# An attention and MoE kernel: the rational activation as a float16 product and a residual, an addition on ScalarE, 19 ring tiles, a new order

## The chip, the cores and the metric

The kernel runs on one core of a Trainium2 chip. A run's time is the device time of that core in microseconds. TensorE multiplies matrices, VectorE, ScalarE and GpSimd work on tiles of 128 partitions, SyncE (SP) issues the transfers. In the profile PE is TensorE, DVE VectorE, ACT ScalarE and POOL GpSimd.

## What is computed

```python
# q, k, v: (4 batches, 8 heads, 768, 64); 16 centroids a head
mask = argmax(q_n @ c_n) == argmax(k_n @ c_n)        # clusters by cosine
attn = softmax(where(mask, q @ k.T / 8, -1e9))
x = (attn @ v) as 3072 tokens x 512
h = x @ w_in                                         # 512 -> 2048
P = a[0] + a[1] * h + a[2] * h**2 + a[3] * h**3
Q = 1 + abs(b[0]) * abs(h) + abs(b[1]) * h**2
out = (P / (Q + 1e-6)) @ w_out                       # 2048 -> 512
```

## The kernel before

Matrix products run in float16 with each operand split in a high and a low part, three products for one. The first of four batches does its attention with the keys as rows; the other three do it by query tile: `attend` takes 128 queries of one head at a time (144 times in all). TensorE makes the scores (L1162), VectorE scales them and takes the extreme (L1191), ScalarE exponentiates, VectorE and ScalarE split the normalised weights into two float16 parts (the split on VectorE is L1222), a transfer on SP's queue turns them, and TensorE multiplies by v into `px` (L1242).

`moe` works on 256 tokens at a time (three such blocks in a batch) and on 512 columns of d_ff in two halves. One half is a MoE tile: 128 partitions by 512 elements, 96 of them in all, 72 in the first three batches. For each, TensorE makes `ph` (L1450, 24 matmuls in two steps), and the engines then make the activation in three float32 tiles u, t and s:

- ScalarE: u = |ph| scaled, t = a first polynomial step. VectorE: two more steps (L1467, L1468); the constant term a0 is still missing in t.
- GpSimd: s = u + BT (L1515), s = s * u (L1516); s is Q without its 1.
- ScalarE: in three tiles of four s = s + cq and then u = Ln(s), in the others u = Ln(s + cq); u = Exp(-u), an estimate of 1/Q.
- s = s * u with cq added, near 1: GpSimd (L1533 where cq is not in yet, L1538) in the first three batches, VectorE (L1527) in the last.
- t = (t + a0) * u: GpSimd as two instructions (L1544, L1545) in 43 of the 72 tiles, else VectorE (L1551).
- t = (s - 2) * t on VectorE (L1556): one Newton step for the quotient, with the sign turned.
- ScalarE copies t to float16, the high part (L1560); the low part is the difference, on GpSimd (L1564) in the first three batches and on VectorE in the last. Both parts overwrite s.
- TensorE: `po` += both parts times `wout` (L1575), 12 matmuls in two steps, one for each 128 tokens.

The tiles come from a ring of 12 buffers of 2 KB a partition (`wide`, tag "ring", `NR`), which the preparation of the weights uses as well (`weights`: raw words, magnitudes, signs). In the last batch the second half of each tile pair uses other buffers (`sq1`, `sk1`, `sq2`). A buffer is free again when its last reader is done. No run-time scheduler orders the work: each operation is appended to a plan with an engine, a duration and a due time, and a list written out in the file, `ORDER`, says in which order the plan's operations are issued:

```python
    def emit(self):
        assert sorted(ORDER) == list(range(len(self.ops)))
        for i in ORDER:
            self.ops[i]()
```

An engine takes its own instructions in that order and waits at each for what it needs. Shares such as 0.6 in the table `K` are spread evenly over the tiles by `kshare`.

Of the kernel before, what the change touches and what calls it, by code (L numbers as in the profile page):

```python
# [11 lines left out]
F16 = mybir.dt.float16  # L12
# [3 lines left out]
ALU = mybir.AluOpType  # L16
# [41 lines left out]
K = {'mulp': 0.6, 'mulp.3': 0.0, 'a0t': 1.15, 'xn': 14, 'scp': 1, 'vsc': 0.75, 'sup0': 0, 'stk': 2, 'lop': 0, 'mgp': 0, 'rvn': 2, 'at': 3, 'vn': 3, 'ah': 5, 'sqd': 0.0, 'ed': 0.0, 'ed.3': 1.0, 'gld': 0.0, 'gld.3': 1.0, 'sqd.3': 0.0, 'ghd': 0.0, 'sua': 1.0, 'acq': 0.75, 'T1': 1, 'quick': 1}  # L58
# [188 lines left out]
def clustered_attention_moe_kernel(  # L247
# [550 lines left out]
    def g_scale(b, vt):  # L798
# [9 lines left out]
        def g1c(i):  # L808
            return g1.ap[:, i : i + 1]
# [600 lines left out]
    def moe(b, tb, vt):  # L1410
# [7 lines left out]
        for ci in range(NWC):  # L1418
# [11 lines left out]
            for h in range(2):  # L1430
# [61 lines left out]
                def g16(i, sv=sv, k=k):  # L1492
                    w = 2 * TW * (k + 1)
                    return sv().bitcast(F16)[:, i * w : (i + 1) * w]
# [171 lines left out]
```

## Time and profile before

| | |
|---|---|
| median of 3 runs | 931.77 us (931.6 to 931.96) |
| span of the profiled execution | 930.4 us, 1.4 below the median |
| PE busy | 863.5 us, 93% |
| DVE busy | 835.6 us, 90% |
| ACT busy | 811.2 us, 87% |
| POOL busy | 729.3 us, 78% |

The span runs from the first to the last instruction; what lies around it is known only as the difference to the runs. Busy shares are means over stages that differ much, so the rows below are split by stage. A busy time contains waits inside an instruction, which matters for instructions whose length varies.

### The profile page before, as it was taken

How to read it: one execution, taken by the hardware profiler on the slowest of the kernel's cores; microseconds unless marked ns; L12 is line 12 of the kernel's file. 1: busy time of each engine (PE TensorE's matmuls, PEld its weight loads, DVE VectorE, ACT ScalarE, POOL GpSimd, SP SyncE). 2: the span in 40 equal slices, each digit the busy share in tenths (PEclk: the TensorE clock that was granted, in tenths of full speed). 3: DMA queues.
4: the chain of work that ended last, by engine and by line, in shares of the span. 5: the costliest groups of instructions: out<-in, count | busy, mean ns of one | idle time of the engine just before them, and what ended most of it. 6: DMA issues, size and time to landing. Idle time of an engine off the chain costs nothing.

```text
span 930.4 us, 20764 instructions
## 1 busy us (share of the span) xinstructions
PE 863.5 (93%) x7705; PEld 581.1 (62%) x7705; DVE 835.6 (90%) x1503; ACT 811.2 (87%) x1558; POOL 729.3 (78%) x771
## 2 busy tenths in 40 slices
PE   1679998988899999999989999999999999999997
PEld 1357665656566666666666766666666675777663
DVE  6789999769989999999999999999999998899986
ACT  5577697989999999999999999999999998886774
POOL 2546789988999999999989988988989996464342
PEclk9989999989999999999999999999999999999999
DMA  7995765796977899998799879896987587501000
GB/s 200 232 249 130 190 193 148 177 230 138 188 133 154 164 161 203 155 167 163 155 162 180 164 135 169 178 188 110 208 150 150 92 165 130 121 2 33 8 24 23
DMA packets 360853, 137.70 MB, mean 148 GB/s; under 512 B 335665, under 2 KB 352049, under 8 KB 360753
## 3 DMA queue, kind: packets, MB, share of 16 engines
q1 hardware_dynamic: 360752, 136.39, 72.0%
q8 instruction: 60, 0.98, 0.4%
q14 instruction: 41, 0.33, 0.1%
HBM read 41.98 MB, written 6.29 MB: 52 GB/s over the span
## 4 chain that ended last, share of the span: by engine, by line
PE 54%; DVE 19%; ACT 9%; POOL 6%; issue 6%; DMA 5%; SPq 1%; ACTq 0%; DVEq 0%; POOLq 0%
PE ph L1450 18%; PE po L1575 18%; PE s L1162 7%; PE px L1242 5%; DVE ah L1222 3%; DVE s L1191 3%; DMA rvm<-in_v_dram 2%; PE s L1286 2%; DVE t L1467 1%; DVE t L1556 1%; ACT s L395 1%; PE px L1349 1%; DVE t L1468 1%; DVE top L1295 1%; PE z L1330 1%
## 5 line engine op out<-in xcount | busy, mean ns | idle before, releaser
L1450 PE MATMUL ph<-x,win 128*128 128x256 f16 x2304 | 273.1, 273 | 6.3 <-DVE t L1468 4.7
L1450 PEld LDWEIGHTS <-win 128*128 128x128 f16 x2304 | 223.2, 98 | 55.3 <-DVE t L1468 8.6
L1575 PE MATMUL po<-wout,s 128*128 128x512 f16 x1008 | 239.3, 379 | 0.7 <-POOL s L1564 0.7
L1191 DVE TENSOR_SCALAR_CACHE_REDUCE s<-s,cc 128x768 f32<-128x768 f32 x144 | 145.9, 1017 | 15.4 <-PE s L1162 14.8
L1575 PEld LDWEIGHTS <-s 128*128 128x128 f16 x1008 | 96.4, 98 | 101.2 <-issue 2.2
L1222 DVE SCALAR_TENSOR_TENSOR ah<-s,su,ah 128x768 f16<-128x768 f32 x144 | 144.9, 1011 | 5.6 <-ACT ah L395 5.3
L395 ACT ACTIVATE ah<-s,su 128x768 f16<-128x768 f32 x144 | 129.0, 901 | 7.8 <-DVE su L1210 7.2
L395 ACT ACTIVATE s<-s,nm 128x768 f32<-128x768 f32 x144 | 126.1, 876 | 7.3 <-DVE s L1191 4.9
L1162 PE MATMUL s<-sk,sq 128*128 128x384 f16 x576 | 117.8, 329 | 8.9 <-DVE ah L1222 7.9
L1516 POOL TENSOR_TENSOR s<-s,u 128x512 f32<-128x512 f32 x84 | 114.4, 1362 | 7.0
L1538 POOL TENSOR_TENSOR s<-s,u 128x512 f32<-128x512 f32 x72 | 99.1, 1378 | 7.0 <-ACT u L395 6.7
L1515 POOL TENSOR_SCALAR s<-u,g 128x512 f32<-128x512 f32 x84 | 69.6, 829 | 36.4 <-ACT u L395 33.6
L1564 POOL TENSOR_TENSOR s<-t,s 128x512 f16<-128x512 f32 x72 | 88.1, 1226 | 8.8 <-ACT s L1560 6.8
L1162 PEld LDWEIGHTS <-sq 128*128 128x128 f16 x576 | 52.2, 98 | 53.7 <-DVE ah L1222 17.9
L1556 DVE SCALAR_TENSOR_TENSOR t<-s,t 128x512 f32<-128x512 f32 x84 | 81.8, 973 | 0.8 <-POOL s L1538 0.5
L1242 PE MATMUL px<-at,vhi 128*64 128x256 f16 x864 | 75.2, 276 | 0.0
L395 ACT ACTIVATE u<-ph,gk 128x512 f32<-128x512 f32 x84 | 57.8, 688 | 9.3 <-PE ph L1450 8.7
L1468 DVE SCALAR_TENSOR_TENSOR t<-t,gk,ph 128x512 f32<-128x512 f32 x84 | 62.8, 748 | 3.0
L395 ACT ACTIVATE t<-ph,gk 128x512 f32<-128x512 f32 x84 | 65.4, 780 | 0.0
L1467 DVE SCALAR_TENSOR_TENSOR t<-ph,gk,t 128x512 f32<-128x512 f32 x84 | 62.1, 739 | 1.1 <-ACT t L395 1.0
L1545 POOL TENSOR_TENSOR t<-t,u 128x512 f32<-128x512 f32 x43 | 57.6, 1340 | 3.6
L1242 PE MATMUL px<-at,vlo 128*64 128x256 f16 x432 | 59.7, 273 | 0.0
(232 smaller groups left out, 1751.3 us busy)
## 6 DMA issues: line engine op xcount, KB each, us to landing
rwi<-in_moe_w_in_dram SPq DMA_DIRECT2D x16, 512.0 KB, 4.1
rwo<-in_moe_w_out_dram SPq DMA_DIRECT2D x16, 512.0 KB, 4.4
rk<-in_k_dram SPq DMA_DIRECT2D x32, 192.0 KB, 3.4
rq<-in_q_dram SPq DMA_DIRECT2D x32, 192.0 KB, 3.7
rvm<-in_v_dram SPq DMA_DIRECT2D x16, 384.0 KB, 3.8
rv<-in_v_dram SPq DMA_DIRECT2D x16, 384.0 KB, 4.1
out_dram<-ob SPq DMA_DIRECT2D x24, 256.0 KB, 2.9
sk<-sk SPq DMA_DIRECT2D x12, 192.0 KB, 3.4
```

The costliest lines, as they stand in the source:

```text
L395: lambda: nc.scalar.activation(out=out(), in_=in_(), func=func, **{a: (x() if callable(x) else x) for a, x in kw.items()}),
L1162: nc.tensor.matmul(sc.ap[:, i, :SH], lhsT=st["q" + x].ap[:, j, t, :], rhs=st["k" + x].ap[:, j, ks, :].rearrange("p t c -> p (t c)"), start ...
L1191: lambda nm=nm, view=view: ts(out=view(), in0=view(), scalar1=cc.ap[:, 0:1], scalar2=None, op0=ALU.mult, op1=ALU.min, accum_out=nm.ap),
L1222: lambda part=part, view=view, su=su: stt(out=part(1), in0=view(), scalar=su.ap, in1=part(0), op0=ALU.mult, op1=ALU.subtract),
L1242: nc.tensor.matmul(px.ap[j * D : (j + 1) * D, :], lhsT=vv.ap[:, j, kt, :], rhs=at[j].ap[:, p_, kt].rearrange("p t c -> p (t c)"), start=(i ...
L1450: nc.tensor.matmul(ph.ap[:, fi * TW : (fi + 1) * TW], lhsT=win[:, wpart, c, f * P : (f + 1) * P], rhs=xs[c].ap[:, xpart], start=(i == 0), ...
L1468: stt(out=t[h].ap, in0=t[h].ap, scalar=col("a1")(), in1=ph.ap, op0=ALU.add, op1=ALU.mult)
L1516: nc.gpsimd.tensor_tensor(out=sv(), in0=sv(), in1=uv(), op=ALU.mult)
L1538: lambda uv=uv, sv=sv: nc.gpsimd.tensor_tensor(out=sv(), in0=sv(), in1=uv(), op=ALU.mult),
L1556: lambda tv=tv, sv=sv: stt(out=tv(), in0=sv(), scalar=2.0, in1=tv(), op0=ALU.subtract, op1=ALU.mult),
L1564: lambda tv=tv, g16=g16, e=(nc.vector if kshare("gld", b, i_) else nc.gpsimd): e.tensor_tensor(out=g16(1), in0=tv(), in1=g16(0), op=ALU.su ...
L1575: nc.tensor.matmul(po[ti].ap, lhsT=g16(gg)[:, c0 : c0 + P], rhs=wout[:, wpart, f, :], start=(i == 0 and f == 0), stop=(i == 2 and f == NF ...
```

## The change

The quotient is made in another way. g is a new float16 tile from the ring with a high and a low part (in the last batch's second halves a buffer `sk2`).

- s = u + BT is done by ScalarE in all tiles, s = s * u stays with GpSimd. The separate addition of cq is gone: Ln takes it as its bias everywhere.
- high part at once: g0 = (t + a0) * u, written as float16.
- residual: s = (s + 1 + 1e-6) * g0, then t = (t + a0) - s.
- low part from it: g1 = t * u, on GpSimd in all tiles.
- g0 and t - s are on VectorE in seven tiles of ten; in three of ten GpSimd does them (t + a0, then the product and the difference). The product with g0 is always on VectorE. The shares are the same in all batches.
- the two polynomial steps become two entries of the plan. The factor on the output loses its minus sign.
- `NR` is 19; the scratch for transfers that engines describe in software is cut to 1024 bytes.
- `ORDER` is a new list of 4218 entries, before 4184, over the whole kernel.

```diff
-K = {'mulp': 0.6, 'mulp.3': 0.0, 'a0t': 1.15, 'xn': 14, 'scp': 1, 'vsc': 0.75, 'sup0': 0, 'stk': 2, 'lop': 0, 'mgp': 0, 'rvn': 2, 'at': 3, 'vn': 3, 'ah': 5, 'sqd': 0.0, 'ed': 0.0, 'ed.3': 1.0, 'gld': 0.0, 'gld.3': 1.0, 'sqd.3': 0.0, 'ghd': 0.0, 'sua': 1.0, 'acq': 0.75, 'T1': 1, 'quick': 1}
+K = {'xn': 14, 'scp': 1, 'vsc': 0.75, 'sup0': 0, 'stk': 2, 'lop': 0, 'mgp': 0, 'rvn': 2, 'at': 3, 'vn': 3, 'ah': 5, 'sua': 1.0, 'T1': 1, 'quick': 1, 'sqd': 0.0, 'gld': 0.0, 'gp': 0.3, 'pp': 0.0, 'NR': 19, 'acb': 1.0}
...
-            pts(out=g1c(OI), in0=g1c(OI), scalar1=-1.0 / TOP, scalar2=1.0, op0=ALU.mult, op1=ALU.mult)
+            pts(out=g1c(OI), in0=g1c(OI), scalar1=1.0 / TOP, scalar2=1.0, op0=ALU.mult, op1=ALU.mult)
...
+                    g_t = buf([P, 2, FW], F16, "sk2", f"g{n}", kn("stk", 2)) if last and h else buf([P, 2, FW], F16, "ring", f"g{n}_{h}", NR)
...
+                act(722, uv, sv, AF.Ln, ss, us, uu + kb("ln", b), [s_t, u_t], bias=cq)
+                act(630, uv, uv, AF.Exp, [], us, uu + kb("ln", b), [u_t], scale=-1.0)
+                if kshare("gp", b, i_):
+                    op(
+                        "POOL", 847,
+                        lambda tv=tv, col=col: nc.gpsimd.tensor_scalar(
+                            out=tv(), in0=tv(), scalar1=col("a0")(), scalar2=1.0, op0=ALU.add, op1=ALU.mult
+                        ),
+                        [gk], tss, uu + kb("mul", b) - 0.2, [t_t],
+                    )
+                    op(
+                        "POOL", 1340,
+                        lambda tv=tv, uv=uv, g16=g16: nc.gpsimd.tensor_tensor(out=g16(0), in0=tv(), in1=uv(), op=ALU.mult),
+                        [*us, *tss], [g_t], uu + kb("mul", b), [t_t, u_t],
+                    )
                 else:
                     dve(
+                        919,
+                        lambda tv=tv, uv=uv, col=col, g16=g16: stt(
+                            out=g16(0), in0=tv(), scalar=col("a0")(), in1=uv(), op0=ALU.add, op1=ALU.mult
+                        ),
+                        [*us, *tss, gk], [g_t], uu + kb("mul", b), [t_t, u_t], n=1,
+                    )
...
+                    dve(
+                        800,
+                        lambda sv=sv, g16=g16: stt(out=sv(), in0=sv(), scalar=1.0 + 1e-6, in1=g16(0), op0=ALU.add, op1=ALU.mult),
+                        [g_t], ss, uu + kb("e", b), [s_t], n=1,
+                    )
+                if kshare("gp", b, i_):
+                    op(
+                        "POOL", 1362,
+                        lambda tv=tv, sv=sv: nc.gpsimd.tensor_tensor(out=tv(), in0=tv(), in1=sv(), op=ALU.subtract),
+                        ss, tss, uu + kb("fin", b), [t_t, s_t],
+                    )
+                else:
+                    dve(
+                        920,
+                        lambda tv=tv, sv=sv, col=col: stt(
+                            out=tv(), in0=tv(), scalar=col("a0")(), in1=sv(), op0=ALU.add, op1=ALU.subtract
+                        ),
+                        [*ss, gk], tss, uu + kb("fin", b), [t_t, s_t], n=1,
+                    )
...
+                    lambda tv=tv, uv=uv, g16=g16, e=(nc.vector if kshare("gld", b, i_) else nc.gpsimd): e.tensor_tensor(
+                        out=g16(1), in0=tv(), in1=uv(), op=ALU.mult
                     ),
-                    [*tss, gb[0]], [gb[1]], uu + kb("gl", b), [t_t, s_t],
+                    [*tss, *us], [g_t], uu + kb("gl", b), [t_t, u_t],
...
-    nc = _bacc.Bacc("TRN2", target_bir_lowering=False, num_devices=1)
+    nc = _bacc.Bacc("TRN2", target_bir_lowering=False, num_devices=1, dynamic_dma_scratch_size=1024)
```

Dropped from the diff are the new list and the old forms of the same instructions, which the section on the kernel names.

## Rows read from the trace of the kernel before

**Rows 1.** Busy time by stage: start:end, length, busy us (instructions) of each engine.
```profile
0.00:200.00 200.00, 156.05 (x1757) 108.69 (x1759) 163.79 (x336) 146.24 (x270) 138.82 (x176) 0.97 0.77 193
...
200.00:250.00 50.00, 43.99 (x412) 30.71 (x409) 42.89 (x84) 47.28 (x97) 43.61 (x50) 0.99 0.76 168
...
250.00:500.00 250.00, 243.27 (x2121) 161.63 (x2119) 235.17 (x429) 240.29 (x478) 233.06 (x245) 1.00 0.87 163
...
500.00:775.00 275.00, 270.08 (x2348) 181.59 (x2345) 259.42 (x469) 265.57 (x523) 246.03 (x248) 1.00 0.85 157
...
775.00:846.00 71.00, 70.83 (x553) 49.13 (x550) 63.18 (x97) 59.21 (x107) 36.00 (x30) 1.00 0.35 68
...
846.00:930.40 84.40, 79.25 (x528) 49.36 (x525) 71.13 (x94) 52.65 (x86) 31.77 (x26) 0.99 0.08 24
```

**Rows 2.** Chain that ended last: start us, length us, what; the last 73 us.
```profile
857.44 5.24 PE ph L1450 x48
...
862.68 2.59 PE po L1575 x12
```

**Rows 3.** Timeline of VectorE: start us, length us, the last attention split.
```profile
845.03 1.01 DVE L1222 SCALAR_TENSOR_TENSOR ah<-s,su,ah 128x768 f16<-128x768 f32 x1
```

**Rows 4.** VectorE's groups, 250 to 775 us: count, busy us, mean ns.
```profile
L1222 DVE SCALAR_TENSOR_TENSOR ah<-s,su,ah 128x768 f16<-128x768 f32 x124 | 124.8, 1010 | 3.1 <-ACT ah L395 2.8 <-DMA rq<-in_q_dram 0.2
...
L1556 DVE SCALAR_TENSOR_TENSOR t<-s,t 128x512 f32<-128x512 f32 x66 | 63.3, 959 | 0.6 <-POOL s L1538 0.5
...
L1468 DVE SCALAR_TENSOR_TENSOR t<-t,gk,ph 128x512 f32<-128x512 f32 x66 | 49.4, 748 | 2.3
...
L1551 DVE SCALAR_TENSOR_TENSOR t<-t,gk,u 128x512 f32<-128x512 f32 x27 | 31.3, 1158 | 0.0
```

**Rows 5.** One line's instructions over the span: least, median and longest ns.
```profile
L1551 DVE SCALAR_TENSOR_TENSOR t<-t,gk,u x41: 739/945/2130, 218.5 to 910.7; 128x512 f32<-128x512 f32 x41
...
L1556 DVE SCALAR_TENSOR_TENSOR t<-s,t x84: 670/823/1811, 222.4 to 913.1; 128x512 f32<-128x512 f32 x84
```

**Rows 6.** VectorE's groups with two SBUF operands, 790 to 930.4 us.
```profile
L1556 DVE SCALAR_TENSOR_TENSOR t<-s,t 128x512 f32<-128x512 f32 x12 | 11.9, 991 | 0.1
...
L1551 DVE SCALAR_TENSOR_TENSOR t<-t,gk,u 128x512 f32<-128x512 f32 x12 | 10.9, 912 | 0.0
...
L1564 DVE TENSOR_TENSOR s<-t,s 128x512 f16<-128x512 f32 x12 | 10.7, 895 | 0.0
...
L1527 DVE SCALAR_TENSOR_TENSOR s<-s,u 128x512 f32<-128x512 f32 x12 | 10.4, 865 | 0.7 <-ACT u L395 0.6
...
L1564 DVE TENSOR_TENSOR sq<-sk,sq 128x512 f16<-128x512 f32 x12 | 9.8, 815 | 2.6 <-ACT sq L1560 2.5
...
L1527 DVE SCALAR_TENSOR_TENSOR sq<-sq,sq 128x512 f32<-128x512 f32 x12 | 9.4, 785 | 1.9 <-ACT sq L395 1.9
...
L1551 DVE SCALAR_TENSOR_TENSOR sk<-sk,gk,sq 128x512 f32<-128x512 f32 x12 | 9.4, 780 | 0.0
...
L1556 DVE SCALAR_TENSOR_TENSOR sk<-sq,sk 128x512 f32<-128x512 f32 x12 | 9.3, 777 | 0.2
```

**Rows 7.** ScalarE's groups over the whole span: count, busy us, mean ns.
```profile
L1560 ACT CAST s<-t 128x512 f16<-128x512 f32 x84 | 51.7, 617 | 4.3 <-DVE t L1556 4.2
...
L395 ACT ACTIVATE s<-s,cq 128x512 f32<-128x512 f32 x60 | 43.4, 723 | 3.9 <-POOL s L1516 3.9
```

**Rows 8.** GpSimd's groups, 250 to 775 us: count, busy us, mean ns.
```profile
L1538 POOL TENSOR_TENSOR s<-s,u 128x512 f32<-128x512 f32 x66 | 91.1, 1381 | 7.0 <-ACT u L395 6.7
...
L1516 POOL TENSOR_TENSOR s<-s,u 128x512 f32<-128x512 f32 x66 | 88.7, 1343 | 5.5
...
L1564 POOL TENSOR_TENSOR s<-t,s 128x512 f16<-128x512 f32 x66 | 80.6, 1223 | 7.2 <-ACT s L1560 6.8
...
L1515 POOL TENSOR_SCALAR s<-u,g 128x512 f32<-128x512 f32 x66 | 52.9, 801 | 6.7 <-ACT u L395 4.0 <-ACT su L395 1.6 <-PE po L1575 0.2
...
L1545 POOL TENSOR_TENSOR t<-t,u 128x512 f32<-128x512 f32 x39 | 52.5, 1347 | 3.3
```

More of the change, by code (lines that the diff above doesn't have):

```diff
@@ L1464, in moe @@
                 )
-                def poly(t=t, h=h, ph=ph, col=col):
-                    stt(out=t[h].ap, in0=ph.ap, scalar=col("rho")(), in1=t[h].ap, op0=ALU.mult, op1=ALU.mult)
-                    stt(out=t[h].ap, in0=t[h].ap, scalar=col("a1")(), in1=ph.ap, op0=ALU.add, op1=ALU.mult)
-                dve(1523, poly, [ph, gk], [t[h]], u_ + h + kb("phr", b), [t_t], n=2)
+                dve(
+                    739,
+                    lambda t=t, h=h, ph=ph, col=col: stt(
+                        out=t[h].ap, in0=ph.ap, scalar=col("rho")(), in1=t[h].ap, op0=ALU.mult, op1=ALU.mult
+                    ),
+                    [ph, gk], [t[h]], u_ + h + kb("phr", b), [t_t],
+                )
+                dve(
+                    748,
+                    lambda t=t, h=h, ph=ph, col=col: stt(
+                        out=t[h].ap, in0=t[h].ap, scalar=col("a1")(), in1=ph.ap, op0=ALU.add, op1=ALU.mult
+                    ),
+                    [ph, gk], [t[h]], u_ + h + kb("phr", b), [t_t],
+                )
                 gw = 1 if last and ci >= NWC - 1 and tb >= NB - kn("fine", 0) else GW
@@ L1490, in sv, with g16 @@
                     return view(s_t)
-                def g16(i, sv=sv, k=k):
-                    w = 2 * TW * (k + 1)
-                    return sv().bitcast(F16)[:, i * w : (i + 1) * w]
+                def g16(i, g_t=g_t):
+                    return g_t.ap[:, i]
                 uu = u_ + seg[-1]
-                mulp = kshare("mulp", b, i_)
-                swap = kn("swap") and not last and not mulp
-                if kshare("sqd", b, i_) or swap:
+                if kshare("sqd", b, i_):
                     dve(
@@ L1512, in moe @@
                 else:
-                    def square(uv=uv, sv=sv):
-                        nc.gpsimd.tensor_scalar(out=sv(), in0=uv(), scalar1=g1c(BT), scalar2=1.0, op0=ALU.add, op1=ALU.mult)
-                        nc.gpsimd.tensor_tensor(out=sv(), in0=sv(), in1=uv(), op=ALU.mult)
-                    op("POOL", (2330, 3930)[k], square, [*us, g1], ss, uu + kb("sq", b), [s_t, u_t])
-                acq = kshare("acq", b, i_)
-                if acq:
-                    act((724, 1165)[k], sv, sv, AF.Identity, [], ss, uu + kb("ln", b), [s_t], bias=cq)
@@ L1522, in moe @@
-                act((630, 1070)[k] if acq else (724, 1165)[k], uv, sv, AF.Ln, ss, us, uu + kb("ln", b), [s_t, u_t], **({} if acq else {"bias": cq}))
-                act((630, 1070)[k], uv, uv, AF.Exp, [], us, uu + kb("ln", b), [u_t], scale=-1.0)
-                if kshare("ed", b, i_):
-                    dve(
-                        (840, 1300)[k] if last else (1000, 1850)[k],
-                        lambda uv=uv, sv=sv, acq=acq: stt(out=sv(), in0=sv(), scalar=0.0 if acq else 1.0 + 1e-6, in1=uv(), op0=ALU.add, op1=ALU.mult),
-                        us, ss, uu + kb("e", b), [s_t, u_t], n=1,
-                    )
-                else:
-                    if not acq: op(
-                        "POOL", (790, 1340)[k],
+                    op(
+                        "POOL", 829,
+                        lambda uv=uv, sv=sv: nc.gpsimd.tensor_scalar(
+                            out=sv(), in0=uv(), scalar1=g1c(BT), scalar2=1.0, op0=ALU.add, op1=ALU.mult
+                        ),
+                        [*us, g1], ss, uu + kb("sq", b), [s_t, u_t],
+                    )
@@ new lines, in moe @@
+                    op(
+                        "POOL", 1362,
+                        lambda uv=uv, sv=sv: nc.gpsimd.tensor_tensor(out=sv(), in0=sv(), in1=uv(), op=ALU.mult),
+                        [*us, g1], ss, uu + kb("sq", b), [s_t, u_t],
+                    )
[6 more added lines that the diff above has]
+                            out=tv(), in0=tv(), scalar1=col("a0")(), scalar2=1.0, op0=ALU.add, op1=ALU.mult
+                        ),
+                        [gk], tss, uu + kb("mul", b) - 0.2, [t_t],
+                    )
+                    op(
+                        "POOL", 1340,
+                        lambda tv=tv, uv=uv, g16=g16: nc.gpsimd.tensor_tensor(out=g16(0), in0=tv(), in1=uv(), op=ALU.mult),
+                        [*us, *tss], [g_t], uu + kb("mul", b), [t_t, u_t],
+                    )
+                else:
+                    dve(
+                        919,
+                        lambda tv=tv, uv=uv, col=col, g16=g16: stt(
+                            out=g16(0), in0=tv(), scalar=col("a0")(), in1=uv(), op0=ALU.add, op1=ALU.mult
+                        ),
+                        [*us, *tss, gk], [g_t], uu + kb("mul", b), [t_t, u_t], n=1,
+                    )
@@ L1533, in moe @@
+                if kshare("pp", b, i_):
+                    op(
+                        "POOL", 790,
                         lambda sv=sv: nc.gpsimd.tensor_scalar(out=sv(), in0=sv(), scalar1=cq, scalar2=1.0, op0=ALU.add, op1=ALU.mult),
-                        [], ss, uu + kb("e", b) - 0.5, [s_t],
+                        us, ss, uu + kb("e", b) - 0.5, [s_t],
                     )
                     op(
-                        "POOL", (1360, 2440)[k],
-                        lambda uv=uv, sv=sv: nc.gpsimd.tensor_tensor(out=sv(), in0=sv(), in1=uv(), op=ALU.mult),
@@ L1539, in moe @@
-                        us, ss, uu + kb("e", b), [s_t, u_t],
-                    )
-                if mulp or swap:
-                    def times(tv=tv, uv=uv, col=col):
-                        nc.gpsimd.tensor_scalar(out=tv(), in0=tv(), scalar1=col("a0")(), scalar2=1.0, op0=ALU.add, op1=ALU.mult)
-                        nc.gpsimd.tensor_tensor(out=tv(), in0=tv(), in1=uv(), op=ALU.mult)
-                    op("POOL", (2183, 3840)[k], times, [*us, gk], tss, uu + kb("mul", b), [t_t, u_t])
-                else:
-                    dve(
-                        (919, 1600)[k] if last else (1110, 2100)[k],
-                        lambda tv=tv, uv=uv, col=col: stt(out=tv(), in0=tv(), scalar=col("a0")(), in1=uv(), op0=ALU.add, op1=ALU.mult),
-                        [*us, gk], tss, uu + kb("mul", b), [t_t, u_t], n=1,
-                    )
@@ L1554, in moe @@
-                dve(
-                    (800, 1290)[k] if last else (1080, 1930)[k],
-                    lambda tv=tv, sv=sv: stt(out=tv(), in0=sv(), scalar=2.0, in1=tv(), op0=ALU.subtract, op1=ALU.mult),
-                    ss, tss, uu + kb("fin", b), [t_t, s_t], n=1,
-                )
-                gb = [ss[0], ss[-1]]
-                op("ACT", (619, 1050)[k], lambda tv=tv, g16=g16: nc.scalar.copy(out=g16(0), in_=tv()), tss, [gb[0]],
-                   uu + kb("gh", b), [t_t, s_t], chain="gh")
@@ L1562, in moe @@
-                op(
-                    *(("DVE", (780, 1400)[k]) if kshare("gld", b, i_) else ("POOL", (1231, 2230)[k])),
-                    lambda tv=tv, g16=g16, e=(nc.vector if kshare("gld", b, i_) else nc.gpsimd): e.tensor_tensor(
-                        out=g16(1), in0=tv(), in1=g16(0), op=ALU.subtract
+                        "POOL", 1360,
+                        lambda sv=sv, g16=g16: nc.gpsimd.tensor_tensor(out=sv(), in0=sv(), in1=g16(0), op=ALU.mult),
+                        [g_t], ss, uu + kb("e", b), [s_t],
+                    )
+                else:
+                    dve(
+                        800,
+                        lambda sv=sv, g16=g16: stt(out=sv(), in0=sv(), scalar=1.0 + 1e-6, in1=g16(0), op0=ALU.add, op1=ALU.mult),
+                        [g_t], ss, uu + kb("e", b), [s_t], n=1,
+                    )
@@ new lines, in moe @@
+                if kshare("gp", b, i_):
+                    op(
+                        "POOL", 1362,
+                        lambda tv=tv, sv=sv: nc.gpsimd.tensor_tensor(out=tv(), in0=tv(), in1=sv(), op=ALU.subtract),
+                        ss, tss, uu + kb("fin", b), [t_t, s_t],
+                    )
+                else:
+                    dve(
+                        920,
+                        lambda tv=tv, sv=sv, col=col: stt(
+                            out=tv(), in0=tv(), scalar=col("a0")(), in1=sv(), op0=ALU.add, op1=ALU.subtract
+                        ),
+                        [*ss, gk], tss, uu + kb("fin", b), [t_t, s_t], n=1,
+                    )
@@ L1566, in moe @@
+                op(
+                    *(("DVE", 780) if kshare("gld", b, i_) else ("POOL", 1361)),
+                    lambda tv=tv, uv=uv, g16=g16, e=(nc.vector if kshare("gld", b, i_) else nc.gpsimd): e.tensor_tensor(
+                        out=g16(1), in0=tv(), in1=uv(), op=ALU.mult
                     ),
-                    [*tss, gb[0]], [gb[1]], uu + kb("gl", b), [t_t, s_t],
+                    [*tss, *us], [g_t], uu + kb("gl", b), [t_t, u_t],
                 )
@@ L1581, in moe @@
                     for ti in range(TB):
-                        op("PE", 6 * 216, lambda ti=ti, h=h, second=second: second(ti, h), [*ss, *wo], [po[ti]],
-                           u_ + h + kb("po", b, 4.0), [po2, s_t])
+                        op("PE", 6 * 216, lambda ti=ti, h=h, second=second: second(ti, h), [g_t, *wo], [po[ti]],
+                           u_ + h + kb("po", b, 4.0), [po2])
         whole = load([P, TB, DM], F32, f"ob{b}_{tb}") if MERGE else None
```

364 rows, old and new, of the table ORDER are left out of this document.

## The prediction

> **What bounds the kernel now.** I read the stage windows first [rows 1]. From 250 to 775 us TensorE is busy 513.4 us of 525 (97.8%), from 775 to 846 us 70.8 of 71, after it 79.3 of 84.4. So TensorE sets the pace from about 250 us to the end; ScalarE (505.9 of 525, 96%), VectorE (494.6, 94%) and GpSimd (479.1, 91%) run close behind. Ahead of 250 us TensorE is busy only 200.0 of 250: that is where time could come from. The chain that ended last confirms the end: in the last 70 us it is first and second product in turn, 12 matmuls of `ph` in 1.31 us (48 in 5.24) and 6 of `po` in 1.30 (12 in 2.59) [rows 2]. The chain also gives what one step of TensorE's queue is worth. One more point in time matters: the last attention split on VectorE starts at 845.03 us and takes 1.01, so ends at 846 [rows 3]. Behind it stand the last turn of the weights, the last `px`, and then only MoE steps on TensorE: 84.4 us to the end of the span.
>
> VectorE's rows in the middle [rows 4] show that it does two different kinds of work. Instructions with a PSUM operand do not vary (L1222 1010 ns, L1468 748). Those with two SBUF operands do: L1551 has a least time of 739 ns and L1556 of 670 [rows 5], but their means in the middle are 1158 and 959 [rows 4]. The excess, 0.42 us in 27 and 0.29 us in 66 instructions, is 0.33 us a piece. In the last stage the eight groups with two SBUF operands have means of 0.777 to 0.991 us [rows 6]; over the same least times (739 for L1551, 670 for the rest) the excess is 0.165 us a piece. GpSimd is busy 91% in the middle and 67.8 of 155.4 us (44%) from 775 us on [rows 1]: the excess goes with GpSimd's share. I call it w.
>
> **ScalarE: less work.** A copy of 617 ns goes from all 96 tiles, and an Identity add of cq (723 ns) from 72 of them; an Identity add of BT comes to all 96, which I take at the same 723 [rows 7]: 59 + 52 - 69 = 42 us less over the span, from which the bias that Ln takes again in those 72 tiles gives a little back. ScalarE is not what ends last, so I count this as no gain: TensorE and VectorE hide it. If both had room, it would give up to 42 us.
>
> **GpSimd: much less in the middle.** Per 66 middle tiles go L1515 (52.9 us) and L1538 (91.1), and the pair of L1545 (39 by 1.347, with an add ahead of each like L1515's 0.801: 83.8 together) falls to 19 of 66 tiles (three in ten), each with a third instruction of 1.35 us [rows 8]. L1516 and L1564's 1223 ns stay in kind. 479.1 - 52.9 - 91.1 - 42.9 + 25.7 = 318, 61% of 525. Cost nothing; it lowers w.
>
> **VectorE: more work, and this sets the sum.** Before, a middle tile has L1551 in 29 of 72 and L1556 in all. After, it has the product into g in 51, the product with g in 72, and the residual in 51; tile number i leaves two of them to GpSimd by the 0.3 share (21 of 72 in the first three batches, 7 of 24 in the last). All three have two SBUF operands. The last batch loses L1527, L1551, L1556 and L1564's subtraction on VectorE and gets the same three. I count what stands in VectorE's own order ahead of the last attention split, in the old list and in the new one. Old: 29 x 1.158 + 72 x 0.959 in the first three batches, 32 of the last batch at 0.85 (mean of the groups in [rows 6]): 33.6 + 69.0 + 27.3 = 129.9 us. New: 110 with a column as scalar (L1551's kind, at least 0.739) and 79 with a constant (L1556's, at least 0.670): 81.3 + 52.9 = 134.2 us, plus 189 w. One tile less has its two polynomial steps ahead (1.5 us). So 2.8 us + 189 w more. No row shows the float16 output and input of these forms on VectorE beyond L1564's, which has the same least time class [rows 6]; I take no gain. Bounds for w: 0.165 (GpSimd at 44%) and 0.33 (at 91%); 61% is nearer the first, so I take 0.17: +32, together +35 us.
>
> The Trainium skill, SBUF — State Buffer, section Who interferes with whom, says that a VectorE instruction with two SBUF inputs and a GpSimd instruction that reads SBUF exclude each other, the second waiting until the first is done. By that rule every hit would cost half a GpSimd instruction of 1.35 us, at 61% about 0.41 us a piece, and the sum would be some 45 us above mine. The trace agrees in kind (a longest L1556 of 1811 ns [rows 5]), but at 91% the rule would give 0.62 and the row gives 0.33.
>
> **The order.** In TensorE's list 41 steps of `po` and 22 of `ph` follow the last attention product, where 33 and 20 did: 8 x 1.30 + 2 x 1.31 = 13.0 us more behind the split [rows 2]. So 97.4 us instead of 84.4. The same attention work therefore has to be done earlier while VectorE has more to do. The steps ahead of the first MoE tile are 171 on TensorE where they were 170, and about the same work on VectorE and ScalarE; SP's queue issues the same transfers, shuffled with the rest, so I price its moves at nothing, covered by TensorE's 2% and by VectorE's backlog; if a transfer comes late, it adds to VectorE's idle time below.
>
> **The ring and the waits.** 19 tiles against 12 hold four tiles per MoE tile instead of three: 4.75 in flight for 4. g is freed by `po`, the others earlier. New waits: `po` needs GpSimd's last product in the last batch, where VectorE made it; queued behind that on GpSimd is the next tile's s*u, for which ScalarE's Ln waits. With GpSimd at 44% before in that stage I take 0; if it is late, 1 or 2 us at the end. The ring also feeds the weights; VectorE's idle 36.2 us ahead of 200 and 7.1 us from 200 to 250 [rows 1] may shrink: I take 30 and 4, an estimate.
>
> **The sum.** VectorE is busy 764.5 us up to 846, its first five stages added [rows 1]; its idle time there is 81.5, of which 38.2 lie behind 250 us. If VectorE is what others wait for, I give it the idle share that TensorE has now where it binds, 2% of 600: 12 us, so 46 in all. 764.5 + 35 + 46 = 845.5, then 97.4: a span of 943. The median of the runs lies 1.4 us above the profiled span (931.77 against 930.4): **944 us**. TensorE alone would give 846 - 13 + 97.4, the old span: it no longer binds.
>
> **Rivals.**
> - *VectorE becomes the bound* (forecast), 0.55. With w of 0.165 and 35 us idle 932; with 0.25 and 50 us 963. For it: 94% busy in the middle now, and 189 dearer instructions. Against: the 82 us of idle it had.
> - *TensorE stays the bound and starts earlier*, faster, 0.27. The place is 150 to 250 us, where weights and first tiles share the ring; TensorE's gaps ahead of 250 us are 50 us, and a quarter of them back gives 930.4 - 12.5 + 1.4 = 919. It decides where 189 w plus idle stays under 64 us: w under 0.10 at 46 us idle, or 0.16 at 33. For it: 0.165 was seen late in the span; against: at least 30 us of idle belong to the start, when data arrive.
> - *The changes cancel*, 0.08: less from the start, more on VectorE, or ScalarE and GpSimd eased where TensorE bound anyway. 930 to 934.
> - *The port wait stays as in the middle now*, 0.10: w 0.33 gives 189 x 0.33 = 62 instead of 32, so 974. For it: two-operand instructions now follow each other, and so do GpSimd's of 1.35 us. This is the rule above in a softer form; in full it would give 990.
>
> Chances: slower by over 0.2% 0.52 + 0.10 = 0.62; within 0.2% (about what a measurement here can tell from no change) 0.09; faster 0.29. For 8 in 10 the range goes from 915 (most of the faster rival) to 968 (part of the last). The forecast's own range is 932 to 963.
>
> **What would show it.** Right: VectorE over 97% busy from 250 us to the last split, that split at 840 to 855 us, TensorE's idle time waiting for VectorE (`po` or scores behind products with g), GpSimd near 60% and ScalarE near 91% in the middle; means near 0.85 us for the product with g and 0.91 for the other two. Wrong: means near 0.68 and 0.74, or VectorE idle under 35 us ahead of the split, or TensorE full from before 230 us. The prediction fails most easily on w and on how early the first MoE tile starts.

## The result, and the profile after

915.6 us (four runs, 914.8 to 917.3) against 931.7 before (four runs): a ratio of 0.9856, 95% interval 0.9822 to 0.9890 (the two medians alone give 0.983). The change makes the kernel faster by 1.4%; the forecast was 944 us and slower. The profiled span is 913.0 us. Runs of the kernel before spread more than those of after, from 926.7 to 932.0 us over all chips used, and its profiled span of 930.4 us lies at the slow end; that matters for the start, below.

Busy time by stage of the kernel after, in the columns of [rows 1], cut at its own last attention split:

```profile
0.00:200.00 200.00, 159.20 (x1877) 114.10 (x1877) 157.50 (x343) 150.99 (x282) 126.72 (x164) 0.97 0.81 198
...
200.00:250.00 50.00, 44.76 (x403) 32.04 (x404) 47.71 (x90) 49.07 (x93) 42.63 (x46) 1.00 0.81 146
...
250.00:500.00 250.00, 246.59 (x2176) 168.98 (x2174) 245.62 (x483) 243.93 (x476) 153.69 (x159) 1.00 0.93 176
...
500.00:775.00 275.00, 269.78 (x2313) 181.54 (x2311) 264.90 (x498) 254.99 (x491) 161.66 (x169) 1.00 0.84 154
...
775.00:818.50 43.50, 43.50 (x358) 32.87 (x356) 37.82 (x54) 39.98 (x69) 27.08 (x22) 1.00 0.26 53
...
818.50:913.00 94.50, 90.18 (x586) 55.42 (x584) 66.58 (x74) 51.77 (x80) 64.78 (x48) 0.99 0.08 25
```

One line's instructions over the span, least, median and longest ns, then first and last start:

```profile
L1224 DVE SCALAR_TENSOR_TENSOR ah<-s,su,ah x144: 990/1009/1020, 195.7 to 817.5; 128x768 f16<-128x768 f32 x144
```

The last split ends at 818.5 us, where it ended at 846 [rows 3], and 94.5 us follow. In the middle TensorE is busy 516.4 us of 525 (before 513.4 [rows 1]), VectorE 510.5 (97.2%, before 494.6), ScalarE 498.9, GpSimd 315.4 (60%, before 479.1). VectorE has indeed hardly any idle time left there. But up to the last split it is busy only 753.5 us, 11 less than before, and not 35 more.

VectorE's three new forms in the middle, 250 to 775 us (count, busy us, mean ns):

```profile
L1572 DVE SCALAR_TENSOR_TENSOR s<-s,g 128x512 f32<-128x512 f32 x68 | 48.6, 715 | 0.2
...
L1553 DVE SCALAR_TENSOR_TENSOR g<-t,gk,u 128x512 f16<-128x512 f32 x47 | 38.1, 810 | 0.0
...
L1584 DVE SCALAR_TENSOR_TENSOR t<-t,gk,s 128x512 f32<-128x512 f32 x47 | 35.0, 747 | 0.3
```

Over the least times of [rows 5] (739 ns with a column as scalar, 670 with a constant) that is 0.07, 0.05 and 0.01 us: 0.04 us a piece, where [rows 4] gave 0.33. From 775 us to the end the same forms look quite different:

```profile
L1572 DVE SCALAR_TENSOR_TENSOR s<-s,g 128x512 f32<-128x512 f32 x12 | 13.2, 1100 | 0.5
...
L1584 DVE SCALAR_TENSOR_TENSOR t<-t,gk,s 128x512 f32<-128x512 f32 x11 | 13.2, 1196 | 0.2
...
L1553 DVE SCALAR_TENSOR_TENSOR g<-t,gk,u 128x512 f16<-128x512 f32 x10 | 12.0, 1201 | 4.1 <-ACT u L397 3.9
...
L1572 DVE SCALAR_TENSOR_TENSOR sq<-sq,g 128x512 f32<-128x512 f32 x12 | 10.9, 908 | 6.3 <-POOL g L1547 5.7
...
L1584 DVE SCALAR_TENSOR_TENSOR sk<-sk,gk,sq 128x512 f32<-128x512 f32 x7 | 6.3, 905 | 0.2
...
L1553 DVE SCALAR_TENSOR_TENSOR g<-sk,gk,sq 128x512 f16<-128x512 f32 x7 | 5.9, 844 | 3.1 <-PE po L1602 2.3 <-ACT sq L397 0.6
```

Here the excess is 0.33 us a piece, at a GpSimd share of 67% (91.9 of 138). Who waited longest for whom in the middle (us in total, times, longest):

```profile
POOL g L1591 <- DVE t L1584: 67.2, 26, 5.2
...
POOL t L1578 <- DVE s L1572: 22.7, 7, 6.6
...
PEld L1164 <- DVE ah L1224: 14.8, 30, 2.2
...
PE s L1164 <- DVE ah L1224: 5.8, 7, 1.7
```

GpSimd now waits for VectorE: 67 us for the residual, 23 for the product with g. TensorE's matmuls wait for the attention split for 6 us in all and its weight loads (PEld), which run beside matmuls, for 15; before these were 7 and 15, so the gain does not show in these waits.

How far TensorE got can be estimated: the matmuls of nine groups by stage, times what one takes in an unbroken run (0.109 us for `ph`, 0.216 for `po`, and so on). In us of work done by the time in the first column; the second kernel with the old order is the run with only the ring changed (below, profiled span 926.6):

```
by us   before   old order, 19 ring tiles   after   after - second
200      124.7            131.4             131.6        0.2
250      166.7            172.2             175.8        3.6
325      239.7            244.9             250.5        5.6
450      361.3            367.2             373.4        6.2
600      506.9            511.7             524.1       12.4
775      680.6            685.3             696.0       10.7
```

So the lead of 7 us at 200 us that the two profiles show comes neither from the new quotient nor from the new order: the old order with 19 ring tiles has it too. Whether the ring or the single execution makes it, one trace of each cannot tell; in the time the ring alone gives nothing (below), which speaks for the execution. What quotient and order give comes from 200 us on: 3.6 us to 250 and some 9 more to 600. By this estimate TensorE did 97.0% of what it could there (339.5 of 350, the old order with 19 ring tiles), and now does 99.5% (348.3).

### The profile page after: what moved, and what is told of

The parts are those of the page before. It is cut to its first block, busy times and chain, and to the rows that moved or that the text cites. A ratio compares the mean times of both kernels' runs of the same rounds, so it can differ in the third digit from the quotient of the medians.

```text
span 913.0 us, 20529 instructions
## 1 busy us (share of the span) xinstructions
PE 854.0 (94%) x7705; PEld 584.9 (64%) x7705; DVE 820.1 (90%) x1538; ACT 790.7 (87%) x1486; POOL 576.6 (63%) x607
## 4 chain that ended last, share of the span: by engine, by line
PE 53%; DVE 15%; ACT 15%; DMA 9%; issue 5%; SPq 1%; POOL 1%; ACTq 0%; DVEq 0%
PE po L1602 18%; PE ph L1453 17%; PE s L1164 6%; PE px L1244 5%; ACT s L397 4%; DMA sq<-tq 3%; DVE s L1193 3%; ACT ah L397 2%; ACT u L397 2%; DVE ah L1224 2%; DMA rvm<-in_v_dram 2%; PE z L1332 1%; ACT t L397 1%; DVE g L1553 1%; PE ptl L1060 1%
## 5 line engine op out<-in xcount | busy, mean ns | idle before, releaser
L1602 PE MATMUL po<-wout,g 128*128 128x512 f16 x1152 | 266.7, 379 | 0.5 <-POOL g L1591 0.3
L1453 PE MATMUL ph<-x,win 128*128 128x256 f16 x2304 | 266.3, 273 | 0.6 <-DVE df L1075 0.4
L1602 PEld LDWEIGHTS <-g 128*128 128x128 f16 x1152 | 111.2, 98 | 121.3 <-issue 2.2
L1591 POOL TENSOR_TENSOR g<-t,u 128x512 f16<-128x512 f32 x84 | 117.6, 1402 | 97.1 <-DVE t L1584 81.1
L1518 POOL TENSOR_TENSOR s<-s,u 128x512 f32<-128x512 f32 x84 | 112.5, 1344 | 49.5 <-ACT s L397 38.8
L1164 PE MATMUL s<-sk,sq 128*128 128x384 f16 x576 | 114.2, 326 | 11.7 <-DVE ah L1224 9.2
L1572 DVE SCALAR_TENSOR_TENSOR s<-s,g 128x512 f32<-128x512 f32 x84 | 64.6, 769 | 0.7
L397 ACT ACTIVATE s<-u,g 128x512 f32<-128x512 f32 x84 | 60.6, 724 | 1.1 <-POOL t L1578 0.3
L397 ACT ACTIVATE u<-s,cq 128x512 f32<-128x512 f32 x84 | 59.7, 718 | 1.7 <-POOL s L1518 1.7
L1553 DVE SCALAR_TENSOR_TENSOR g<-t,gk,u 128x512 f16<-128x512 f32 x61 | 53.5, 878 | 4.1 <-ACT u L397 3.9
```

The costliest lines, as they stand in the source:

```text
L397: lambda: nc.scalar.activation(out=out(), in_=in_(), func=func, **{a: (x() if callable(x) else x) for a, x in kw.items()}),
L1164: nc.tensor.matmul(sc.ap[:, i, :SH], lhsT=st["q" + x].ap[:, j, t, :], rhs=st["k" + x].ap[:, j, ks, :].rearrange("p t c -> p (t c)"), start ...
L1453: nc.tensor.matmul(ph.ap[:, fi * TW : (fi + 1) * TW], lhsT=win[:, wpart, c, f * P : (f + 1) * P], rhs=xs[c].ap[:, xpart], start=(i == 0), ...
L1518: lambda uv=uv, sv=sv: nc.gpsimd.tensor_tensor(out=sv(), in0=sv(), in1=uv(), op=ALU.mult),
L1553: lambda tv=tv, uv=uv, col=col, g16=g16: stt(out=g16(0), in0=tv(), scalar=col("a0")(), in1=uv(), op0=ALU.add, op1=ALU.mult),
L1572: lambda sv=sv, g16=g16: stt(out=sv(), in0=sv(), scalar=1.0 + 1e-6, in1=g16(0), op0=ALU.add, op1=ALU.mult),
```

## The experiments

All ratios are to the kernel before, run on the same chip; after stands at 0.9856.

**The old quotient in the new order.** The parts of the old quotient get a tile of their own (`g_t`, as in the change), 19 ring tiles; each old operation is issued where the new one stands that does its part. Against the kernel before, without the list:

```diff
+                    g_t = buf([P, 2, FW], F16, "sk2", f"g{n}", kn("stk", 2)) if last and h else buf([P, 2, FW], F16, "ring", f"g{n}_{h}", NR)
...
-                def g16(i, sv=sv, k=k):
-                    w = 2 * TW * (k + 1)
-                    return sv().bitcast(F16)[:, i * w : (i + 1) * w]
+                def g16(i, g_t=g_t):
+                    return g_t.ap[:, i]
```

> The old quotient (copy and Newton step, GpSimd's shares as before), with its high and low part in a tile of their own, 19 ring tiles, and the new order carried over to its operations. Theory O (the gain comes from the order, which lets TensorE start earlier between 150 and 250 us and keeps it fed): about 918 us. Theory Q (the gain comes from the relief that the new quotient gives GpSimd, ScalarE and the shared port): 930 us or more, GpSimd and ScalarE again over 90% busy in the middle.

1123 us, ratio 1.210 (1.2075 to 1.2127). Waits between 250 and 775 us:

```profile
ACT g L1560 <- DVE t L1556: 59.0, 31, 4.8
...
POOL g L1564 <- ACT g L1560: 83.2, 32, 9.7
```

**The new quotient in the old order**, 19 ring tiles, the other way round.

> The new quotient and 19 ring tiles in the old order (each new operation stands where the one stood that it takes the place of). Theory O: about 931 us or slower, because VectorE has its three operations in places made for others. Theory Q: 918 to 922 us.

1001 us, ratio 1.078 (1.0762 to 1.0806).

```profile
POOL s L1517 <- ACT s L396: 187.4, 56, 8.3
...
PE s L1163 <- DVE ah L1223: 36.2, 41, 3.8
```

Neither theory holds: with the wrong partner, either half costs far more than the whole change brings. The rows show where engines stand. In the first, ScalarE waits at its copy for the Newton step (59 us) and GpSimd for that copy (83 us). In the second, ScalarE's new addition has been put where GpSimd's square stood, GpSimd waits 187 us for it, and TensorE waits 36 us for the attention split, where it waited 7 before. Which of these waits carries the loss was not traced. An order written out fits one set of operations; as carried over, these two runs cannot split the gain.

**19 ring tiles alone** in the kernel before.

```diff
-... 'T1': 1, 'quick': 1}
+... 'T1': 1, 'quick': 1, 'NR': 19}
-    nc = _bacc.Bacc("TRN2", target_bir_lowering=False, num_devices=1)
+    nc = _bacc.Bacc("TRN2", target_bir_lowering=False, num_devices=1, dynamic_dma_scratch_size=1024)
```

> The kernel before with 19 ring tiles and the small scratch, nothing else. If waits for a free ring tile held TensorE or the weights in the old order, 925 to 929 us; if not (both theories), 931 us, no change over 0.2%.

928.6 us, ratio 1.0003 (0.9988 to 1.0019): nothing. Smaller rings under the new order were not timed.

**The new front on the old kernel, the old front on the new one.** Nearly all of the entries ahead of the first MoE operation (920 in the old list, 917 in the new) are the same operations, so this stretch can be exchanged. In short, where the file has the sorted list written out:

```
front = sorted(ORDER[:920], key=place_in_the_new_order)
ORDER = front + ORDER[920:]
```

> The kernel before (old quotient, 19 ring tiles), of whose order only the 920 entries ahead of the first MoE operation (weights, first batch's attention, first work on the second) are sorted as in the new order; the rest keeps its old order. Theory F (a good part of the gain is won ahead of 250 us by the new order of that stretch alone): 919 to 924 us, with scores and first MoE tiles 5 to 8 us earlier. Theory M (it is won where MoE tiles run, by the matched quotient and order): 929 to 932 us.

938.3 us, ratio 1.0107 (1.0091 to 1.0123).

> The kernel after with the 917 entries ahead of its first MoE operation sorted as in the old order, all else as after. Theory F: 921 to 925 us, the lead of TensorE at 250 us gone. Theory M: 914 to 917 us.

917.8 us, ratio 0.9880 (0.9858 to 0.9901). Busy time of the first 200 us, old kernel with new front, then new kernel with old front:

```profile
0.00:200.00 200.00, 158.49 (x1877) 113.68 (x1878) 156.48 (x341) 148.93 (x277) 130.06 (x168) 0.97 0.82 197
```

```profile
0.00:200.00 200.00, 157.74 (x1873) 111.31 (x1873) 162.76 (x344) 150.44 (x281) 134.15 (x170) 0.98 0.78 198
```

The front is worth at most some 2 us in the new kernel (the intervals of 0.9880 and 0.9856 overlap) and loses 10 in the old one, so Theory F falls, and with it the rival of the prediction in the place that it named: most of the gain is not made ahead of 250 us. One thing this pair does show: the order alone changes how long VectorE is busy with the same work. In the first 200 us it is busy 156.5 us in the old kernel with the new front, where it was 163.8 [rows 1], and 162.8 in the new kernel with the old front, where it was 157.5. The 64 instructions of L544 and L551, which prepare the weights, take 49.6 us in the kernel before and 48.1 with 19 ring tiles; it is 42.6 in the old kernel with the new front, 45.9 in the new kernel with the old front and 42.1 in the kernel after.

**More work for GpSimd.** One spare multiplication behind the low part; as a control two fills; then the multiplication behind s * u.

```diff
                def glow(tv=tv, uv=uv, g16=g16):
                    nc.gpsimd.tensor_tensor(out=g16(1), in0=tv(), in1=uv(), op=ALU.mult)
+                    if b < B - 1:
+                        nc.gpsimd.tensor_tensor(out=junkp, in0=junkp, in1=junkp, op=ALU.mult)
```

> The kernel after with one more GpSimd multiplication (128x512 float32, three times the same spare tile) behind the low part in each of the 72 tiles of the first three batches: GpSimd about 75% busy in the middle. Theory S (the excess of VectorE's two-operand instructions goes with GpSimd's busy share): the three forms' excess rises from 0.06 to 0.2 us or more, VectorE has some 25 us more to do, 930 us or more. Theory D (the excess is low since GpSimd now starts when VectorE's result is ready, so they take turns): the spare instructions start behind that and collide with what VectorE does next; 0.1 to 0.15 us, 918 to 925 us.

> The control to the run with the extra multiplication: in the same places two fills of the spare tile, which write and read nothing, of about the same length together. If what VectorE waits for is GpSimd's reading, the three forms keep their excess of about 0.06 us; the time then shows what GpSimd's longer queue alone costs: 914 to 918 us if nothing.

> The same extra GpSimd multiplication as behind the low part, in the same 72 tiles, but behind s times u: GpSimd's share in the middle is the same 73%. Theory S (the excess of VectorE's two-operand instructions goes with GpSimd's share): 0.12 us a piece as there. Theory D (it goes with where the order puts GpSimd's work against VectorE's): another excess, 0.05 us or more away from 0.12. The time is open: ScalarE's Ln does not wait for the extra instruction, the low part of the tile before does.

In this order: 942.6 us (1.0158, 1.0134 to 1.0182), 936.3 (1.0085, 1.0068 to 1.0101) and 939.4 (1.0112, 1.0084 to 1.0140). The middle of the first, and the three forms:

```profile
250.00:775.00 525.00, 497.75 (x4272) 333.45 (x4270) 503.05 (x935) 479.19 (x920) 382.58 (x382) 0.99 0.84 158
```

```profile
L1574 DVE SCALAR_TENSOR_TENSOR s<-s,g 128x512 f32<-128x512 f32 x64 | 54.2, 848 | 0.1
...
L1555 DVE SCALAR_TENSOR_TENSOR g<-t,gk,u 128x512 f16<-128x512 f32 x43 | 36.6, 851 | 0.1
...
L1586 DVE SCALAR_TENSOR_TENSOR t<-t,gk,s 128x512 f32<-128x512 f32 x44 | 35.0, 797 | 0.2
```

The control with fills:

```profile
250.00:775.00 525.00, 500.58 (x4304) 335.54 (x4301) 503.83 (x946) 483.18 (x932) 373.03 (x449) 1.00 0.85 160
```

```profile
L1574 DVE SCALAR_TENSOR_TENSOR s<-s,g 128x512 f32<-128x512 f32 x64 | 52.0, 812 | 0.6 <-POOL g L1549 0.5
...
L1555 DVE SCALAR_TENSOR_TENSOR g<-t,gk,u 128x512 f16<-128x512 f32 x45 | 39.9, 887 | 0.1
...
L1586 DVE SCALAR_TENSOR_TENSOR t<-t,gk,s 128x512 f32<-128x512 f32 x45 | 35.1, 782 | 0.2
```

The multiplication behind s * u:

```profile
250.00:775.00 525.00, 502.39 (x4352) 336.73 (x4351) 510.00 (x945) 485.94 (x935) 384.65 (x387) 1.00 0.85 160
```

```profile
L1577 DVE SCALAR_TENSOR_TENSOR s<-s,g 128x512 f32<-128x512 f32 x63 | 55.2, 877 | 1.1 <-POOL g L1552 1.0
...
L1558 DVE SCALAR_TENSOR_TENSOR g<-t,gk,u 128x512 f16<-128x512 f32 x45 | 38.9, 864 | 0.1
...
L1589 DVE SCALAR_TENSOR_TENSOR t<-t,gk,s 128x512 f32<-128x512 f32 x44 | 36.8, 839 | 0.2
```

With GpSimd at 73% the excess is 0.12 us a piece, within what Theory D had said of that run, though the time (942.6) is beyond D's range. At the same share, with the multiplication in the other place, it is 0.15: nearer to S than D asked for. And the fills, which read nothing, raise it nearly as much (0.11, GpSimd at 71%), so the control missed as well, and it is not only the spare instruction's own reading that VectorE meets. For each of the three forms in the middle (and for the two old forms in the kernel before) the trace gives which GpSimd instruction was running when it started:

```
                      none running    tensor with tensor    others    excess when tensor with tensor ran    share of time with one running
before (old forms)       9 of 93            53                31          0.49 us                              64%
after                  129 of 162           25                 8          0.19 us                              50%
spare multiplication    84 of 151           51                16          0.35 us                              61%
fills                   93 of 154           39                22          0.39 us                              47%
multiplication early    86 of 152           52                14          0.42 us                              62%
```

With nothing running the mean excess is 0.01 us or less in all five. Of the nine instructions that started during a fill, eight lost 0.01 us or less; the ninth lost 1.09, and a GpSimd multiplication began 15 ns after it. So the fills cost VectorE nothing while they run: they push GpSimd's own multiplications into its way.

What one meeting costs can be read instruction by instruction, as in these two pairs of the last run (start us, length us):

```profile
279.67 1.27 POOL L1520 TENSOR_TENSOR s<-s,u 128x512 f32<-128x512 f32 x1
...
280.52 0.97 DVE L1558 SCALAR_TENSOR_TENSOR g<-t,gk,u 128x512 f16<-128x512 f32 x1
...
518.68 1.26 POOL L1520 TENSOR_TENSOR s<-s,u 128x512 f32<-128x512 f32 x1
...
519.00 1.49 DVE L1577 SCALAR_TENSOR_TENSOR s<-s,g 128x512 f32<-128x512 f32 x1
```

In the first, 0.42 us of GpSimd's instruction are left and VectorE's is 0.23 longer than its least time; in the second 0.94 are left and it is 0.82 longer. In 146 of the 148 cases of the five runs with 0.25 us or more left, VectorE lost what was left less 0.11 to 0.20 us. So the excess has two factors: how many instructions start while GpSimd runs such an instruction, and how much of it is then left. Neither is GpSimd's share of busy time.

All three runs also cost more time than VectorE's longer instructions: the first has 0.08 us x 190 = 15 us more of them and takes 28 us more.

**More work for VectorE** (72 times a maximum over spare numbers; 0.343 us a piece, 24.7 us in all, not the 19 expected).

```diff
...
+                        plan.ops[-1] = lambda f=last_fn: (f(), nc.vector.tensor_reduce(out=junkr, in_=junkp, axis=AX.X, op=ALU.max))
```

> The kernel after with one more VectorE instruction behind the product with g in each of the 72 tiles of the first three batches: a maximum over 192 spare numbers, about 0.26 us, one SBUF operand, which nobody waits for: some 19 us more on VectorE. Theory V (VectorE, 97% busy, sets the pace of the middle together with TensorE): nearly all of it is seen, 12 to 19 us more than after, 928 to 935 us. Theory T (TensorE alone sets it, the rest has slack): at most 6 us more, 916 to 922 us.

929.6 us, ratio 1.0019 (1.0005 to 1.0034): 15 us more than after.

```profile
250.00:775.00 525.00, 508.56 (x4376) 339.35 (x4374) 515.55 (x1022) 492.44 (x944) 310.70 (x324) 1.00 0.87 162
```

```profile
L1227 DVE SCALAR_TENSOR_TENSOR ah<-s,su,ah x144: 990/1008/1019, 194.8 to 831.2; 128x768 f16<-128x768 f32 x144
```

VectorE is 98.2% busy, the last split comes 13.7 us later and the span ends 13.8 later. The 24.7 us are lengths of instructions; VectorE's busy time ahead of the split grew by 18.9 us (772.4 against 753.5), since the records of neighbouring instructions overlap. Of that, 15 us are seen in the time: Theory V, rather than T.

**More work for ScalarE.**

```diff
                 act(630, uv, uv, AF.Exp, [], us, uu + kb("ln", b), [u_t], scale=-1.0)
...
+                    plan.ops[-1] = lambda f=last_fn, uv=uv: (f(), nc.scalar.copy(out=junkh, in_=uv()))
```

> The kernel after with the float16 copy of a tile put back on ScalarE, 0.62 us in each of the 72 tiles of the first three batches (of u, behind the exponential; nobody reads it): 44 us more on ScalarE, which the prediction had counted as hidden. Hidden work (the prediction's step): 916 to 920 us. Theory R (ScalarE's relief is needed by the new pace, as it was 96% busy before and is 95% now): ScalarE full, 930 us or more.

949.8 us, ratio 1.0236 (1.0213 to 1.0259): 35 us more than after, for 44.5 us of work. As Theory R had it, ScalarE is full (97%):

```profile
250.00:775.00 525.00, 493.49 (x4230) 329.31 (x4230) 487.78 (x928) 509.82 (x978) 299.09 (x317) 1.00 0.83 157
```

```profile
L1225 DVE SCALAR_TENSOR_TENSOR ah<-s,su,ah x144: 986/1010/1020, 195.4 to 851.7; 128x768 f16<-128x768 f32 x144
```

**The addition back on GpSimd.**

```diff
-... 'acb': 1.0}
+... 'acb': 0.0}
```

> The kernel after with the addition of BT back on GpSimd (0.83 us in 96 tiles) and off ScalarE (0.72 us), in the same places of the order. If GpSimd's longer queue costs what the fills showed (0.28 us for each us put on it in the first three batches): 15 us or more slower than after, 930 us. If ScalarE's work is what counts: faster than after, 905 to 913 us.

954.7 us, ratio 1.0279 (1.0258 to 1.0300), 39 us more than after, though ScalarE falls to 86% busy:

```profile
250.00:775.00 525.00, 501.74 (x4364) 337.61 (x4362) 512.97 (x947) 452.87 (x871) 357.06 (x388) 1.00 0.85 160
```

```profile
L1224 DVE SCALAR_TENSOR_TENSOR ah<-s,su,ah x144: 985/1007/1019, 198.0 to 849.6; 128x768 f16<-128x768 f32 x144
```

**Fewer tiles on GpSimd.**

```diff
-                if kshare("gp", b, i_):
+                gp = kshare("gp", b, i_) and not (b < B - 1 and (i_ // 10) % 2)
...
+                if gp:
```

> The kernel after with 9 of the 21 tiles, whose product into g and residual GpSimd makes in the first three batches, given to VectorE: about 14 us more on VectorE, 30 us less on GpSimd. If VectorE sets the pace: 920 to 930 us. If GpSimd's queue does: 908 to 914 us.

951.2 us, ratio 1.0245 (1.0213 to 1.0276): 36 us more for 14 us of work moved to VectorE, beyond both bounds.

```profile
250.00:775.00 525.00, 492.27 (x4218) 331.74 (x4216) 495.99 (x942) 473.88 (x912) 270.05 (x288) 0.98 0.83 155
```

```profile
POOL g L1594 <- DVE t L1587: 97.3, 28, 9.9
...
PE po L1605 <- POOL g L1594: 13.2, 3, 6.3
```

VectorE is not even full (94%). GpSimd waits 97 us for the residual, where it waited 67, and TensorE 13 us for the low part. VectorE's product into g now stands where GpSimd's stood; that this place is wrong for it would fit, but was not tested. This run says more on the order than on either engine.

## Why the prediction was wrong

**The frame held.** The prediction took the end of the span as VectorE's queue up to the last attention split, plus about 97 us of MoE steps on TensorE. After: 818.5 + 94.5. With more for VectorE 832.2 + 94.6, with more for ScalarE 852.7 + 94.6; in all six runs that add or move work in the first three batches alone the tail is 94.5 or 94.6 us, and the end moved with the split. (With the addition back on GpSimd, in the last batch too, the tail is 104.1.) VectorE did reach 97%, as forecast, GpSimd 60% where 61% was worked out, and the addition of work to VectorE is mostly seen in the time. 190 of the new instructions stand ahead of the split (189 counted).

**The step that failed is VectorE's work ahead of the split**: 764.5 + 35 = 799.5 us forecast, 753.5 measured.
- The term 189 w: w was taken as 0.17 from a row of the last stage, on the ground that the excess goes with GpSimd's share. The three forms took 147.0 us ahead of the split; the least times of 134.9 leave 12.1, so 0.064 a piece: 20 us too much. The share is no measure for it: 0.04 us at 60% in the middle, 0.33 at 67% at the end of the same execution. In the middle 25 of 162 started while GpSimd ran a tensor-with-tensor instruction, though one was running half of the time, and lost 0.19 us each; from 775 us on it is 24 of 59, and 0.67 us each. The prediction's own sign of being wrong, means near 0.68 and 0.74, is close to what came in the middle: 0.715, 0.810 and 0.747. Why they meet so seldom there was not shown. That GpSimd waits for VectorE's results and VectorE then turns to work with a PSUM operand fits, and the run that moved the spare multiplication spoke rather against place as the only cause. Within the middle, more GpSimd work added to this order did bring part of the excess back (0.11 to 0.15 at 71 to 73%).
- The prediction let VectorE's other instructions stand. Ahead of the split they took 17 us less, beyond the tile whose steps it had counted: 7.6 in the preparation of the weights (L544 and L551 of before), 4.5 in the low parts of q and k (L1010), the rest in many small ones. The exchanged fronts show that the order of the front moves most of the first part, and none of the second. The old forms took 131.5 us where 129.9 were worked out: 2 more.
- The prediction added lengths of instructions to a busy time. But in these traces the record of one instruction starts a little before that of the one ahead ends: up to the split VectorE's lengths add up to 853.2 us before and 850.5 after, its busy time is 764.5 and 753.5. So 88.8 us of overlap became 97.0, with 1411 instructions and then 1465: 8 us of added length that are no busy time. The same holds for ScalarE, whose lengths fell by 38 us over the span and its busy time by 20.5 (811.2 to 790.7), where the prediction had 42; it is 95% busy in the middle, not near 91%.

With one instruction more than counted (0.7 us back), these make up the 46 us.

Of the two other terms, VectorE's idle time was off the other way: 65.0 us, not 46 (42.5 of it ahead of 200 us, where 30 were taken). The tail is 94.5, not 97.4. 943 - 46 + 19 - 3 = 913.

**ScalarE's relief counted as nothing** was wrong for the new order, though it has no term: the copy put back costs 35 us. That is the price in an order made without the copy; what the copy would cost in an order made with it, no run shows. With VectorE at 94% and ScalarE at 96% before, that relief of one and a new order for the rest were worth something to TensorE, which had to be read as 97%, not as full, fits the runs and is not shown by them.

**The rival** (TensorE stays the bound and starts earlier, 919 us) came within 4 us of the time, in part by luck: the gain lies mostly not ahead of 250 us, but in TensorE's small stalls from 250 to 600. Where it took 12.5 us back ahead of 250, the table has 9.1, and 5.5 of these (172.2 - 166.7) the old order with 19 ring tiles has too, without being faster than the kernel before. Its condition, 189 w plus idle time under 64 us, was not met either (12 + 65): VectorE was done in time because its other work took less. How the gain divides between quotient and order, and so its cause, is open: each without the other is slower than before, and no run holds a good order for either half.

**The Trainium skill's rule** on the shared port (SBUF — State Buffer, section Who interferes with whom: a VectorE instruction with two SBUF inputs and a GpSimd instruction that reads SBUF exclude each other, and the later one waits for the end of the other) agrees with the trace: a mean excess of 0.01 us or less without a running GpSimd instruction, and what was left of GpSimd's instruction, less 0.11 to 0.20 us, in 146 of 148 cases with 0.25 us or more left. It says what a meeting costs. How many there are was the question; here that changed with the order and with the work added to it.

## What to carry to other kernels

When the engines are nearly full, a wait at a shared port has to be priced by how often the two instructions meet and how much of the other one is then left, not by how busy the other engine is; a stage with other neighbours gives no price. Lengths of instructions are not to be added to a busy time where their records overlap. Where the order is written out by hand or by a planner, operations and order are one thing: exchange one without the other and the loss (here 8 and 21%) hides what either is worth. Adding a little work to one engine at a time gives a price for each: here 0.8 us of time for each us on ScalarE, 0.6 on VectorE, and 0.3 on GpSimd, though GpSimd was busy only 60%. In an order made for other work none of it was free, so such a price does not say by itself which engine sets the pace.

## What was not expected of the hardware

In five runs the observed forms of VectorE with two SBUF operands took their least time, to 0.01 us in the mean, when GpSimd ran nothing at their start. When a GpSimd tensor-with-tensor instruction ran they lost 0.19 to 0.49 us on average, and one by one what was left of it less 0.11 to 0.20 us. Cases with under 0.25 us left lost 0.11 us or less, but for five that lost 1.05 to 1.11: there GpSimd's next such instruction began within 0.04 us of VectorE's start. A fill of 0.525 us cost nothing by itself (eight of nine cases). Two executions of the old order, one with 12 and one with 19 ring tiles, differed by 6.7 us in the work that TensorE had done by 200 us (124.7 and 131.4), though their runs have the same median (928.6 and 928.7 us on one chip); whether the ring or the execution makes that difference was not shown.
